# Gated mix of two attentions on one core: half sums of keys formed before the projection stretch, row halves six products apart, small copies on GpSimd, first weight loads ahead

## The chip, the cores and the metric

The kernel runs on one core of a Trainium2 chip. The metric is the device time in microseconds of one execution; lower is better. The engines are TensorE (PE in the profile, with PEld for its weight loads), VectorE (DVE), ScalarE (ACT), GpSimd (POOL) and the queue engine SyncE (SP). Each works through its own instructions in order, and waits on semaphores for the others.

## The reference

Both branches read the same x (2048 x 512) and have 32 heads of 16 columns. Branch A looks at 8 keys per query, at distances 0, 2, .. 14. Branch B has one head of keys and values for all 32 query heads, and looks at all 2048 keys.

```python
g = sigmoid((x * gate_w).sum(-1))
# A: qkv = x @ wqkv; logits over idx = pos - [0, 2, .. 14], masked below 0
a = softmax(q . k[idx] * scale) . v[idx] @ wo_a
# B: q = x @ wq (32 heads), k = x @ wk, v = x @ wv (one head)
b = softmax(q k^T * scale) v @ wo_b
out = g * a + (1 - g) * b
```

All arrays are float32. Products that need the accuracy are made of three float32r products of high and low parts.

## The kernel before

**Two row halves.** Most products have 64 rows of contraction or fewer. TensorE then works as two halves, rows 0 to 63 and rows 64 to 127, which run side by side: a product in one half and a product in the other take the time of one. Instructions are issued in one order, so a product that waits holds back those behind it in both halves.

**Start, to about 24 us.** x is loaded and split into high (`xh`, ACT) and low parts (`xl`, DVE; for the second quarter of x on POOL, `split_x(1, nc.gpsimd)`). `keys(t)` makes the keys, values and gate logits of four blocks of 512 rows in 128-row products; keys land in `kst`, and a turned copy in `turned_k` for values and gates. Two query lumps are made here, too. After it `values_of` copies pieces of `turned_k` into `vst` and `gate`: 16 pairs of small copies (L251 and L253), on ACT.

**The front stretch, 24 to 279 us (`front_stream`).** 62 lumps, 14 of queries (`queries`) and 48 of branch A's projection (`a_project`), of 12 products in each row half (L1212), accumulate into four banks `pe`. A finished bank is read by ACT: L277 and L278 for queries (`qraw`, `qhi`), L315 for branch A (`stage`). The weights of branch A come in pieces: `load_wa` issues a DMA on the POOL queue into one of two `waraw` buffers (L168), ACT makes the high part (`wah`, L119), POOL the low part (`wal`, L179).

**Max products.** The softmax of branch B subtracts the true row maximum, so all scores are made once for their maxima: 2048 products of 128 queries by 512 keys, in 32 units of 64. `max_mm` (L382) makes scores, and DVE reduces them into the tile `mx` of the unit (L420 for a pair over bank `pm`, L432 for one in bank `ps` or `po`). `unit_tile` clears the `mx` of this unit and the next, in the front on ACT (L376). The other way goes through half sums: `half_keys` (L460, 128-row products with the selector `sel`) makes half the sum and half the difference of two key blocks, ACT and DVE put them into `kcd` (L468, L472). Then max(a, b) is the half sum plus the size of the half difference: a product with the difference into `pm` is read by ACT (L511, Abs into `dd`), a product with the sum into `ps` or `po` (L481) by one DVE instruction that adds `dd` and keeps the maximum (L529). It takes as many products on TensorE and less of DVE. Before, `half_sel` builds `sel` on DVE at the eighth query lump, and `half_keys` runs for both groups of keys after it.

**The loop, 282 to 1434 us.** 512 steps (32 units of 16 key tiles). A step has two exponent pairs (`exp_pair`, two products side by side at L574, one ACT exponential of 128 x 1024 at L576) and one group of weighted sums (`weighted`, L584, four tiles of 32 columns, two passes each). Max products that the front left over go into the steps: a pair over `pm` in nearly every step, and a single one in `ps` in some. At steps 272 and 416 come blocks of output rows (`out_phase`), with more max products among them.

**What sets the order.** The kernel is recorded by a planner in Python: it keeps a clock for each engine (`clk`), adds fixed costs (`T_R` for a product slot, `T_RED1`, `T_RED2` and others for what reads a bank), and places a max product when its bank is free by that clock. In the loop `single_share` spreads what is left evenly. `FRONT` (596) ends new half-sum groups in the front when so many max products are done. What a wait really costs is not in the plan.

```python
elif at[b] < n * many and may(b, *lines[b][at[b]]):
    mm(b, lines[b][at[b]])
```

Of the kernel before, what the change touches and what calls it, by code (L numbers as in the profile page):

```python
# [13 lines left out]
P = 128  # L14
# [33 lines left out]
WB = 6  # L48


T_R, T_LAT, T_EXP, T_RED2, T_RED1, T_W, T_TTR = 0.23, 0.20, 0.92, 1.14, 0.61, 1.21, 0.70
# [34 lines left out]
def gated_mix_kernel(ctx, tc, xt, wa, wk, wq, wo_a, wo_b, out):  # L86
# [40 lines left out]
    def after(eng, ready, dur):  # L127
        clk[eng] = max(clk[eng], ready) + dur
        return clk[eng]
# [91 lines left out]
    nc.vector.memset(mk[:, 6:7], -FMAX)  # L221
    clear(0, nc.vector)
# [25 lines left out]
    def values_of(t, q):  # L248

        v = turned_k[32:64, t].rearrange("p (j b z) -> p j b z", b=4, z=32)[:, :, q, DH:2 * DH]  # L250
        nc.scalar.activation(vst[32 * q:32 * q + 32, 4 * t:4 * t + 4, 0:DH], v, AF.Copy)  # L251
        g = turned_k[96:128, t].rearrange("p (j b z) -> p j b z", b=4, z=32)[:, :, q, DH]
        nc.scalar.activation(gate[32 * q:32 * q + 32, 1, 4 * t:4 * t + 4], g, AF.Copy)  # L253
        after("act", clk["pe"], 0.45)
# [56 lines left out]
    def a_post(gg, j, bank):  # L311

        settle("store", 2)
        own = p1.tile([P, GN], F32, name="stage", bufs=4)
        nc.scalar.activation(own, bank, AF.Copy)  # L315
        at = after("act", clk["pe"] + T_LAT, 0.52)

        def store():
            for piece in a_pieces(gg):
                a_store(own, gg, j, *piece)  # L320

        tasks.append((at + 0.5, store, (), "store"))
        if j == NJ - 1:
            tasks.append((at + 1.0, whole, (gg,)))
# [32 lines left out]
    slots = [(0, pr, t, kc) for kc in range(2) for pr in range(2) for t in range(4)]  # L357
    slots += [(0, pr, t, kc) for pr in range(2) for t in range(4) for kc in range(2, 4)]
# [78 lines left out]
    sel, dd, formed, ended, wants = [], [], {}, set(), []  # L437
    hb = {}

    def half_sel():  # L440

        whole_k = wp.tile([P, 2, DH], F32, name="wholek", bufs=1)
        nc.vector.tensor_add(whole_k, twin[:, :, 0, :, 0], twin[:, :, 0, :, 1])
        sel.append(p0.tile([P, 2, P], F32R, name="sel", tag="wkh", bufs=1))
        dd.extend(p1.tile([P, 2, 512], F32, name="dd", bufs=2) for _ in range(2))
        for x in range(2):
            to = sel[0][:, x].rearrange("p (b h z) -> p b h z", b=2, h=2)
            nc.vector.tensor_scalar(to[:, :, 0].rearrange("p b (d s) -> p b d s", s=2), whole_k.unsqueeze(3).to_broadcast([P, 2, DH, 2]), 0.5 - x, 0.0, op0=ALU.mult, op1=ALU.add)
            nc.vector.tensor_scalar(to[:, :, 1].rearrange("p b (s d) -> p b s d", s=2), whole_k.unsqueeze(2).to_broadcast([P, 2, 2, DH]), 0.5 - x, 0.0, op0=ALU.mult, op1=ALU.add)
        after("dve", 0, 1.0)  # L450

    def half_keys(g):

        hb[g] = (m2.shape(2)[:, 0, :], m2[:, 1, :])
        keys = ("m2", "m2")
        clk["pe"] = max(clk["pe"], free["m2"])
        mark("m20", "m21")
        for x in range(2):
            for y in range(2):
                nc.tensor.matmul(hb[g][x], sel[0][:, x * y], kst[:, (2 * g + y) * 512:(2 * g + y + 1) * 512], start=(y == 0), stop=(y == 1))  # L460
        clk["pe"] += 1.2
        for k in keys:
            free[k] = clk["pe"] + 4.0
        tasks.append((clk["pe"] + 1.0, half_parts, (g, keys)))

    def half_parts(g, keys):
        for x in range(2):
            nc.scalar.activation(kcd[:, g, x], hb[g][x], AF.Identity, scale=mk[:, 0:1])  # L468
            at = after("act", clk["pe"], 0.65)
        for x in range(2):  # L470
# [724 lines left out]
    def mm(b, at):  # L1195
# [22 lines left out]
    ends_at, posted, first = {}, set(range(-4, 0)), {}  # L1218
# [10 lines left out]
    def front_stream():  # L1229
# [11 lines left out]
        while min(at) < n * many:  # L1241
# [16 lines left out]
            for b in sorted((0, 1), key=lambda b: b not in lone):  # L1258
# [4 lines left out]
                elif at[b] < n * many and may(b, *lines[b][at[b]]):  # L1263
# [3 lines left out]
            if lone or moved:  # L1267
                idle = 0
                after("pe", 0, T_R)
# [65 lines left out]
    free.update({f"f{k}": 0.0 for k in range(4)})  # L1335
    front_stream()
# [172 lines left out]
```

## Time and profile before

| | |
|---|---|
| median of 3 runs | 1445.83 us (1444.48 to 1447.59) |
| the profiled execution, its own time | 1444.96 us |
| its span | 1443.0 us |
| busy in the span: PE, ACT, DVE, POOL | 99%, 90%, 80%, 67% |
| granted TensorE clock | 0.999 |
| start, front stretch, first 256 steps | to 24 us, 24 to 279 us, 282 to 803 us |

The 1.96 us between the span and the time lie outside the recorded instructions. PE counts as busy while any product is in flight, and a product is in flight for about 0.4 us though the next in its half can begin 0.23 us later; so PE at 99% does not say that no product waited. The distance between the starts of products says it.

### The profile page before, as it was taken

Reading aid. Unit: us, or ns where it says so; the run is one execution under the profiler, and the core shown is the slowest. Engines: PE = TensorE matmul, PEld = TensorE weight load, DVE = VectorE, ACT = ScalarE, POOL = GpSimd, SP = SyncE. Lnnn points to the kernel's source line nnn. Section 1 sums busy time; section 2 is a strip of 40 time slices with the busy share of each in tenths; the row PEclk is TensorE's granted clock in tenths of the full one; section 3 lists DMA queues with packets and bytes.
Section 4 is the critical chain, followed back from the end, with each engine's and each line's share of the span. In section 5 each row is a group of like instructions: output and inputs, shape, how many; then the busy total and the mean of one; then the engine's idle time right before and its main releaser. Section 6 shows DMA issues by size and latency. Waiting matters only on the chain.

```text
span 1443.0 us, 29289 instructions
## 1 busy us (share of the span) xinstructions
PE 1432.9 (99%) x10524; PEld 675.9 (47%) x10524; DVE 1152.0 (80%) x1883; ACT 1297.3 (90%) x1649; POOL 963.9 (67%) x1749
## 2 busy tenths in 40 slices
PE   9999999999999999999999999999999999999998
PEld 7877767533333333333333367333333336333343
DVE  8788888788887888888888889788888888788712
ACT  5599888899999999999999988999999998999986
POOL 4541778878898898988988898888888706011220
PEclk9999999999999999999999999999999999999999
DMA  6654533402121110112322210321201011000110
GB/s 228 185 138 111 150 105 91 131 16 87 40 59 48 52 61 2 61 46 68 101 77 67 73 35 31 94 57 42 72 16 69 12 41 35 9 1 2 30 30 30
DMA packets 106969, 94.01 MB, mean 65 GB/s; under 512 B 84880, under 2 KB 89016, under 8 KB 102728
## 3 DMA queue, kind: packets, MB, share of 16 engines
q1 hardware_dynamic: 99864, 52.95, 13.5%
q0 software_dynamic: 6240, 37.89, 8.0%
q8 instruction: 82, 1.34, 0.4%
q10 hardware_dynamic: 720, 1.31, 0.3%
q14 instruction: 63, 0.52, 0.1%
HBM read 62.13 MB, written 29.45 MB: 63 GB/s over the span
## 4 chain that ended last, share of the span: by engine, by line
PE 97%; DMA 1%; ACT 1%; DVE 1%; issue 0%; SPq 0%; POOL 0%; ACTq 0%; POOLq 0%; DVEq 0%
PE po L584 35%; PE pe L574 24%; PE pe L1212 11%; PE pm L382 8%; PE ps L382 5%; PE pe L889 4%; PE pm L481 4%; PE ps L481 2%; PE po L481 2%; PE pm L943 1%; DMA qd<-qhi 0%; ACT pexp L576 0%; PE pe L238 0%; DMA waraw<-wa 0%; PE po L204 0%
## 5 line engine op out<-in xcount | busy, mean ns | idle before, releaser
L576 ACT ACTIVATE pexp<-pe 128x1024 f32<-128x1024 f32 x1022 | 983.2, 1022 | 62.8 <-PE pe L574 60.3
L420 DVE TENSOR_REDUCE mx<-pm 128x2 f32<-128x1024 f32 x486 | 594.9, 1224 | 169.3 <-PE pm L382 162.8
L584 PE MATMUL po<-pexp,vst 128*32 128x512 f32 x4096 | 545.6, 605 | 0.2 <-ACT pexp L576 0.2
L574 PE MATMUL pe<-qst,kst 64*128 64x512 f32 x1788 | 421.7, 455 | 1.7 <-ACT stage L315 0.9
L574 PEld LDWEIGHTS pe<-qst,kst 64*128 64x128 f32 x1788 | 167.6, 183 | 443.7 <-ACT pexp L576 436.6
L432 DVE TENSOR_REDUCE mx<-ps 128x1 f32<-128x512 f32 x303 | 206.2, 681 | 2.6 <-PE ps L382 2.5
L382 PE MATMUL pm<-kst,qst 62*128 62x512 f32 x915 | 186.0, 396 | 0.1
L648 POOL TENSOR_TENSOR pr<-aext 128x256 f32<-128x256 f32 x256 | 181.8, 738 | 4.7 <-DMA aext<-ad 4.5
L711 POOL TENSOR_TENSOR oa<-oa,av 128x256 f32<-128x256 f32 x224 | 164.1, 733 | 15.3
L511 ACT ACTIVATE dd<-pm 128x512 f32<-128x512 f32 x254 | 147.8, 602 | 25.1 <-PE pm L481 5.9
L584 PEld LDWEIGHTS po<-pexp,vst 128*32 128x32 f32 x4096 | 80.7, 108 | 145.2 <-issue 135.8
L708 POOL TENSOR_TENSOR av<-aext,lg 128x256 f32<-128x256 f32 x224 | 139.3, 622 | 12.9
L1212 PE MATMUL pe<-wah,xl 64*128 64x512 f32 x384 | 131.3, 396 | 0.0
L1212 PE MATMUL pe<-wal,xh 64*128 64x512 f32 x384 | 131.0, 395 | 0.0
L1212 PE MATMUL pe<-wah,xh 64*128 64x512 f32 x384 | 129.4, 395 | 0.0
L481 PE MATMUL pm<-kcd,qst 62*128 62x512 f32 x288 | 113.7, 401 | 0.1
L382 PE MATMUL ps<-kst,qst 62*128 62x512 f32 x285 | 112.6, 395 | 0.0
L529 DVE CUSTOM_DVE_ANT_0 dd<-ps,dd 128x512 f32<-128x512 f32 x127 | 87.6, 690 | 17.1 <-PE ps L481 10.1
L529 DVE CUSTOM_DVE_ANT_0 dd<-po,dd 128x512 f32<-128x512 f32 x127 | 87.7, 691 | 11.5 <-PE po L481 7.3
L382 PEld LDWEIGHTS pm<-kst,qst 62*128 62x128 f32 x915 | 88.8, 186 | 2.6 <-DVE mx L420 0.9
L654 POOL TENSOR_TENSOR tr<-pr 128x512 f32<-128x512 f32 x64 | 81.8, 1279 | 4.2
L611 POOL TENSOR_TENSOR rl<-rl,gate_t 128x16 f32<-128x16 f32 x31 | 6.9, 222 | 115.3 <-DVE rl L605 76.0
(205 smaller groups left out, 1997.0 us busy)
## 6 DMA issues: line engine op xcount, KB each, us to landing
aext<-ad POOLq DMA_DIRECT2D x32, 1056.0 KB, 5.5
ad<-stage SPq DMA_DIRECT2D x32, 240.0 KB
qst<-qd SPq DMA_DIRECT2D x56, 128.0 KB
qd<-qhi SPq DMA_DIRECT2D x16, 256.0 KB
qd<-qlo SPq DMA_DIRECT2D x16, 256.0 KB
td<-raw SPq DMA_DIRECT2D x32, 128.0 KB
oa<-td SPq DMA_DIRECT2D x256, 16.0 KB
xraw<-xt SPq DMA_DIRECT2D x15, 256.0 KB
```

The source lines that it names most:

```text
L382: nc.tensor.matmul(dst, qst[home(v)[0]][b:b + 62, pr, t * P:(t + 1) * P], kst[b:b + 62, kc * 512:(kc + 1) * 512], start=True, stop=True)
L420: nc.vector.tensor_reduce(m[:, :, pr, t, kc], dst, AX.X, ALU.max)
L432: nc.vector.tensor_reduce(m[:, odd, pr, t, kc:kc + 1], dst, AX.X, ALU.max)
L481: nc.tensor.matmul(dst, qst[home(v)[0]][b:b + 62, pr, t * P:(t + 1) * P], kcd[b:b + 62, kc // 2, x, :], start=True, stop=True)
L511: nc.scalar.activation(d[:, odd], m2[:, odd, :], AF.Abs)
L529: nc.vector.tensor_tensor_reduce(d[:, odd], dst, d[:, odd], 1.0, -FMAX, ALU.add, ALU.max, m[:, odd, pr, t, kc:kc + 1])
L574: nc.tensor.matmul(bank[:, odd, :], kst[b:b + 64, kt * P:(kt + 1) * P], qst[home(u)[0]][b:b + 64, pr, :], start=True, stop=True)
L576: nc.scalar.activation(e, bank, AF.Exp, scale=SCALE)
L584: nc.tensor.matmul(po[32 * i:32 * i + 32, :], vst[:, kt, :], pexp[s, i // 2][:, i % 2, :], start=(kt == 0), stop=(kt == NJ - 1))
L648: nc.gpsimd.tensor_mul(pr[:, k], q, e[:, o:o + NH, AC:2 * AC])
L711: nc.gpsimd.tensor_add(ao, ao, av)
L1212: nc.tensor.matmul(front_bank(x), l[h], r[h], start=(not second and i == 0), stop=(second and i == 3 * C - 1))
```

## The change

Seven things are changed, all of them in the front stretch or ahead of it.

1. `sel` (now `halves_of`) is built on DVE among the constants at the start, not in the stretch; `half_sel` is gone.
2. `half_keys` is asked for as soon as `front_stream` begins: the group of the first two key blocks stands right behind `keys(3)`, the other follows when `pm` is free. Its two ACT copies are issued with the products, not as a later task. The order of unit 0's max products (`slots`) is arranged to match.
3. Row half 1 begins only when row half 0 is six products ahead (`LAG`).
4. `values_of` copies on POOL, not on ACT; `unit_tile` clears `mx` on POOL, always.
5. The first two weight pieces of branch A are loaded ahead of `front_stream`.
6. A front step counts 0.235 in the plan (`T_F`), where it counted 0.23.
7. A weight group counts as landed when all 16 of its lumps have been stored, in whichever order.

```diff
+LAG = 6
-T_R, T_LAT, ... = 0.23, 0.20, ...
+T_F, T_R, T_LAT, ... = 0.235, 0.23, 0.20, ...
...
     def ahead_wa(gg, k):
-        if 0 <= k < 2 * C and k % 2 == 0:
+        if (4 if gg == 0 else 0) <= k < 2 * C and k % 2 == 0:
             load_wa(gg, k // 2)
...
     nc.vector.memset(mk[:, 6:7], -FMAX)
+    whole_k = cp.tile([P, 2, DH], F32, name="wholek")
+    halves_of = cp.tile([P, 2, P], F32R, name="sel")
+    nc.vector.tensor_add(whole_k, twin[:, :, 0, :, 0], twin[:, :, 0, :, 1])
+    for x in range(2):
...
     clear(0, nc.vector)
...
     def values_of(t, q):
-        nc.scalar.activation(vst[32 * q:32 * q + 32, 4 * t:4 * t + 4, 0:DH], v, AF.Copy)
+        nc.gpsimd.tensor_copy(vst[32 * q:32 * q + 32, 4 * t:4 * t + 4, 0:DH], v)
-        nc.scalar.activation(gate[32 * q:32 * q + 32, 1, 4 * t:4 * t + 4], g, AF.Copy)
-        after("act", clk["pe"], 0.45)
+        nc.gpsimd.tensor_copy(gate[32 * q:32 * q + 32, 1, 4 * t:4 * t + 4], g)
+        pool = max(pool, 1e3 * clk["pe"]) + 500
...
-        if j == NJ - 1:
+        landed[gg] = landed.get(gg, 0) + 1
+        if landed[gg] == NJ:
             tasks.append((at + 1.0, whole, (gg,)))
...
-    slots = [(0, pr, t, kc) for kc in range(2) for pr in range(2) for t in range(4)]
-    slots += [(0, pr, t, kc) for pr in range(2) for t in range(4) for kc in range(2, 4)]
+    slots = [(0, 0, t, 2 * g + kc) for g in range(2) for t in range(2) for kc in range(2)]
+    slots += [(0, pr, t, kc) for pr in range(2) for t in range(4) for kc in range(4) if pr or t > 1]
...
                 mx[x] = wp.tile([P, 2, 2, 4, 4], F32, name="mx", bufs=3)
-                if pe:
-                    nc.gpsimd.memset(mx[x], -FMAX)
-                    charge(250)
-                else:
-                    nc.scalar.activation(mx[x].rearrange("p b i t k -> p (b i t k)"), ident[:, 0:64], AF.Identity, scale=0.0, bias=mk[:, 6:7])
+                nc.gpsimd.memset(mx[x], -FMAX)
+                charge(250)
...
     def half_keys(g):
...
         clk["pe"] += 1.2
-        for k in keys:
-            free[k] = clk["pe"] + 4.0
-        tasks.append((clk["pe"] + 1.0, half_parts, (g, keys)))
-
-    def half_parts(g, keys):
         for x in range(2):
             nc.scalar.activation(kcd[:, g, x], hb[g][x], AF.Identity, scale=mk[:, 0:1])
             at = after("act", clk["pe"], 0.65)
+        for k in keys:
+            free[k] = at + 4.0
+        tasks.append((at, half_parts, (g, keys)))
...
-            if lump == ("q", 9):
-                half_sel()
-            elif lump == ("q", 10):
-                wants.extend((1, 0))
...
-                elif at[b] < n * many and may(b, *lines[b][at[b]]):
+                elif at[b] < n * many and (b == 0 or at[0] >= LAG) and may(b, *lines[b][at[b]]):
...
-                after("pe", 0, T_R)
+                after("pe", 0, T_F)
...
+    dd.extend(p1.tile([P, 2, 512], F32, name="dd", bufs=2) for _ in range(2))
+    wants.extend((0, 1))
+    for c in range(2):
+        load_wa(0, c)
     front_stream()
```

The lines of the changed kernel have other numbers: L382 is L388, L460 is L454, L481 is L476, L1212 is L1203, L123 is L124, L168 is L169.

On POOL, from the end of its clearing at the start on, the kernel before has this (`xl` are the low parts of the second quarter of x, `qlo` those of queries, `waraw` the weight pieces):

```order
L1035 MEMSET vst 128x16x16
L123 TENSOR_TENSOR xl<-xraw,xh 128x512 x4
L283 TENSOR_TENSOR qlo<-qraw,qhi 128x512 x2
L168 DMA waraw<-wa 128x512
L283 TENSOR_TENSOR qlo<-qraw,qhi 128x512 x3
L179 TENSOR_TENSOR wal<-waraw,wah 128x512
L168 DMA waraw<-wa 128x512
```

The changed kernel has this at the same place:

```order
L1030 MEMSET vst 128x16x16
L124 TENSOR_TENSOR xl<-xraw,xh 128x512 x4
L169 DMA waraw<-wa 128x512 x2
L381 MEMSET mx 128x64 x2
L259 COPY vst<-turnedk 32x4x16
L261 COPY gate<-turnedk 32x4
```

Both weight loads moved up to the four `xl`, and the two clears of `mx` and the small copies, which were on ACT, now stand behind them.

On PE, at the beginning of the front stretch, the kernel before has this, the names in brackets being engines that the row waits for (`DMAHW`: a transfer; `pe_95` and `pe_94` are banks of the first two lumps in row half 1 and 0):

```order
L382 MATMUL ps<-kst,qst_77 128x512 [waits DMAHW2_49,DMAHW1_49]
L1212 MATMUL pe_95<-xh,wqh 128x512 [waits Activation_49]
L382 MATMUL pm<-kst,qst_77 128x512
L382 MATMUL pm<-kst,qst_77 128x512 [waits DMAHW4_49,DMAHW3_49]
L382 MATMUL po<-kst,qst_77 128x512
L1212 MATMUL pe_94<-xh,wqh 128x512 [waits DVE_49]
```

In the changed kernel the four products of L454 for the first half sums stand here, and then this follows:

```order
L388 MATMUL ps<-kst,qst_77 128x512 [waits DMAHW2_49,DMAHW1_49]
L388 MATMUL po<-kst,qst_77 128x512 [waits DMAHW4_49,DMAHW3_49]
L1203 MATMUL pe_94<-xh,wqh 128x512 [waits DVE_49,Activation_49]
L1203 MATMUL pe_94<-xl,wqh 128x512
L1203 MATMUL pe_94<-xh,wql 128x512
L1203 MATMUL pe_94<-xh,wqh 128x512
L1203 MATMUL pe_94<-xl,wqh 128x512
L1203 MATMUL pe_94<-xh,wql 128x512
L1203 MATMUL pe_95<-xh,wqh 128x512 [waits Activation_49]
L1203 MATMUL pe_94<-xh,wqh 128x512
L1203 MATMUL pe_95<-xl,wqh 128x512
L388 MATMUL ps<-kst,qst_77 128x512 [waits DVE_49]
```

Six products of row half 0 now run alone, and the second product into `ps` stands some eight slots behind the first. It waits for DVE's reduction of the first one, and that reduction, which waited for PE and ACT, now waits for PE and POOL (the clear of `mx`).

More of the change, by code (lines that the diff above doesn't have):

```diff
@@ L48 @@
 WB = 6
-T_R, T_LAT, T_EXP, T_RED2, T_RED1, T_W, T_TTR = 0.23, 0.20, 0.92, 1.14, 0.61, 1.21, 0.70
+LAG = 6
+T_F, T_R, T_LAT, T_EXP, T_RED2, T_RED1, T_W, T_TTR = 0.235, 0.23, 0.20, 0.92, 1.14, 0.61, 1.21, 0.70
 class Banks:
@@ L434, in fill_one @@
         filled(v, 1)
-    sel, dd, formed, ended, wants = [], [], {}, set(), []
+    dd, formed, ended, wants = [], {}, set(), []
     hb = {}
[L440 to L450, printed above, removed]
     def half_keys(g):
@@ L459, in half_keys @@
             for y in range(2):
-                nc.tensor.matmul(hb[g][x], sel[0][:, x * y], kst[:, (2 * g + y) * 512:(2 * g + y + 1) * 512], start=(y == 0), stop=(y == 1))
+                nc.tensor.matmul(hb[g][x], halves_of[:, x * y], kst[:, (2 * g + y) * 512:(2 * g + y + 1) * 512], start=(y == 0), stop=(y == 1))
         clk["pe"] += 1.2
-        for k in keys:
-            free[k] = clk["pe"] + 4.0
-        tasks.append((clk["pe"] + 1.0, half_parts, (g, keys)))
-    def half_parts(g, keys):
         for x in range(2):
@@ L469, in half_parts @@
             at = after("act", clk["pe"], 0.65)
+        for k in keys:
+            free[k] = at + 4.0
+        tasks.append((at, half_parts, (g, keys)))
+    def half_parts(g, keys):
+        at = clk["pe"]
         for x in range(2):
@@ L1216, in mm @@
         return T_R
-    ends_at, posted, first = {}, set(range(-4, 0)), {}
+    ends_at, posted, first, landed = {}, set(range(-4, 0)), {}, {}
     def front_bank(x):
```

4 lines of the change are left out of this document (added).

## The prediction

> **What bounds the kernel now.** I read the page first, then the busy times by stage, then PE's timeline within the stages, and last the engines that PE waits for.
>
> ```profile
> PE 97%; DMA 1%; ACT 1%; DVE 1%; issue 0%; SPq 0%; POOL 0%; ACTq 0%; POOLq 0%; DVEq 0%
> ```
>
> The chain that ended last is PE's own sequence from one end to the other. So time can only come from two places: fewer product slots, or shorter waits between them. Busy times by stretch (span's start to the left, then sum and count for each engine, clock, DMA):
>
> ```profile
> core 0: us, PE busy (x) PEld busy (x) DVE busy (x) ACT busy (x) POOL busy (x), PEclk, DMA share, GB/s
> 24.00:60.00 36.00, 34.02 (x278) 31.55 (x278) 31.58 (x45) 20.19 (x57) 18.02 (x16) 1.00 0.57 163
> 60.00:100.00 40.00, 39.92 (x326) 30.11 (x326) 31.53 (x85) 31.32 (x65) 21.08 (x22) 1.00 0.54 152
> 100.00:180.00 80.00, 80.00 (x684) 60.69 (x682) 70.39 (x210) 72.60 (x145) 33.58 (x56) 1.00 0.46 127
> 180.00:278.00 98.00, 97.78 (x783) 67.95 (x781) 84.48 (x252) 82.00 (x154) 79.14 (x155) 1.00 0.35 98
> 282.00:803.00 521.00, 521.00 (x3730) 193.86 (x3722) 432.40 (x520) 494.77 (x531) 442.05 (x848) 1.00 0.20 58
> ```
>
> Two products, one in each row half, make a slot. From 100 to 180 us, 684 products are 342 slots, so a slot takes 80 / 342 = 0.234 us; from 180 to 278 us it takes 98 / 391.5 = 0.250 us, though PE counts as busy in both. The difference is waiting inside the stretch. In the loop the starts on PE's timeline tell more (start, duration, line, operands):
>
> ```profile
> 285.69 1.07 PE L584 MATMUL po<-pexp,vst 128*32 128x512 f32 x8
> 286.69 0.50 PE L574 MATMUL pe<-qst,kst 64*128 64x512 f32 x2
> 287.02 0.39 PE L382 MATMUL pm<-kst,held 62*128 62x512 f32 x2
> 287.25 0.40 PE L574 MATMUL pe<-qst,kst 64*128 64x512 f32 x2
> 287.58 1.07 PE L584 MATMUL po<-pexp,vst 128*32 128x512 f32 x8
> ...
> 289.71 1.07 PE L584 MATMUL po<-pexp,vst 128*32 128x512 f32 x8
> ```
>
> A step with only the pair of max products lasts 287.58 - 285.69 = 1.89 us, one with a single product into `ps` on top, the next in the order, 289.71 - 287.58 = 2.13 us. So a single costs 0.24 us, if ACT can follow, which these rows tell:
>
> ```profile
> 401.08 3.84 ACT L576 ACTIVATE pexp<-pe 128x1024 f32<-128x1024 f32 x4 [0.19 <-PE pe L574]
> ```
>
> ```profile
> L576 ACT ACTIVATE pexp<-pe 128x1024 f32<-128x1024 f32 x492 | 472.7, 1022 | 25.1 <-PE pe L574 23.6 <-PE pm L382 0.9
> L678 ACT ACTIVATE lg<-lg 128x128 f32<-128x128 f32 x18 | 5.6, 312 | 0.0
> ```
>
> Four exponentials in a row take 3.84 us, the last of them 1.02; so they follow each other every (3.84 - 1.02) / 3 = 0.94 us, and two per step are 1.88. A step without a single is thus at ACT's pace, too. So far such steps nearly always stand next to one with a single, which gives ACT 0.25 us of slack.
>
> **The change part by part.** The sum is made against the profiled execution, 1444.96 us (its span and 1.96 us around it); it lies 0.87 under the median of the runs, 1445.83.
>
> *Slots of the front.* Counted in the order of both programs, the stretch holds 1488 projection products and 8 half-sum products either way, and 564 max products before, 599 now. I place each product in the first free slot of its half, not ahead of the one issued before it. That makes 1039 slots before and 1060 now, with the four half-sum products that moved to its head: 17.5 slots are the 35 products, the rest are halves left empty by the lead of six. 21 x 0.234 = +4.9 us.
>
> *A new wait at its head.* Now `mx` is cleared on POOL, behind four `xl` and two weight loads:
>
> ```profile
> 13.49 0.33 POOL L1035 MEMSET vst<- 128x256 f32 x1
> 23.44 5.52 POOL L123 TENSOR_TENSOR xl<-xraw,xh 128x512 fp32r<-128x512 f32 x4 [9.61 <-ACT xh L119]
> ...
> 94.86 1.11 POOL L168 DMA_DIRECT2D waraw<-wa  x2
> ```
>
> ```profile
> 26.91 0.66 DVE L432 TENSOR_REDUCE mx<-ps 128x1 f32<-128x512 f32 x1
> ```
>
> Before, ACT cleared both tiles, and DVE, busy with keys until then, began its first reduction at 26.91. Now POOL is through with `xl` at 23.44 + 5.52 = 28.96 and with two loads at 30.07; the clear of 128x64 costs between nothing and the 0.33 of a 128x256 one, I take 0.13. So the first reduction runs from about 30.2 to 30.9. When does PE need it?
>
> ```profile
> 24.18 0.50 PE L382 MATMUL ps<-kst,qst 62*128 62x512 f32 x1
> ...
> 24.52 1.00 PE L382 MATMUL pm<-kst,qst 62*128 62x512 f32 x2
> 25.06 0.49 PE L1212 MATMUL pe<-xh,wqh 64*128 64x512 f32 x1
> ...
> 53.93 1.20 PE L460 MATMUL pm<-kst,sel 128*128 128x512 f32 x4
> 55.05 0.49 PE L382 MATMUL po<-kst,qst 62*128 62x512 f32 x1
> ```
>
> The stretch begins at 24.18. The half-sum products take 55.05 - 53.93 = 1.12, the first two max products one slot, and seven products of row half 0 stand ahead of the second product into `ps`: 24.18 + 1.12 + 8 x 0.234 = 27.2. PE is issued in order, so everything behind that product waits, in both halves, and ACT, DVE and POOL get no new banks: 30.9 - 27.2 = +3.7 us. The bounds are +0.4 (the clear in time, the reduction still at 26.91 to 27.57) and +3.9 (a clear of 0.33).
>
> *Two waits that go.* Row half 0 has two products from 24.18 to 25.06, 0.88 us where two slots are 0.47; the product between waits for a transfer of `qst`. Now half-sum products fill this time: -0.4. The other wait:
>
> ```profile
> 57.13 0.63 ACT L119 ACTIVATE wah<-waraw 128x512 fp32r<-128x512 f32 x1 [2.89 <-DMA waraw<-wa]
> ...
> 58.79 0.50 PE L1212 MATMUL pe<-xh,wqh 64*128 64x512 f32 x1 [1.83 <-ACT qhi L278]
> ```
>
> ACT waits for the second weight piece until 57.13, with the copies of a finished bank queued behind, and PE stands still for 1.83 us. Now the load of that piece is issued by 30.07: -1.8. The third and fourth piece still wait for a buffer, but stand several ACT copies ahead of their use. Front: 4.9 + 3.7 - 0.4 - 1.8 = +6.4 us.
>
> *Small copies, `sel`, `half_keys` tasks.* Taken at nothing. The cover for `sel` on DVE at the start is a wait:
>
> ```profile
> 7.73 0.69 DVE L123 TENSOR_TENSOR xl<-xraw,xh 128x512 fp32r<-128x512 f32 x1 [1.17 <-ACT xh L119]
> ```
>
> ```profile
> L449 DVE TENSOR_SCALAR sel<-wholek 128x64 fp32r<-128x64 f32 x1 | 0.2, 190 | 0.0
> ```
>
> Four such and a smaller one are under 1 us, and DVE waits 1.17 us for x before 7.73; without that cover they would delay the low parts of x by 1 us. The copies:
>
> ```profile
> L511 ACT ACTIVATE dd<-pm 128x512 f32<-128x512 f32 x37 | 21.3, 603 | 2.7 <-PE pm L481 0.9 <-PE pe L1212 0.4
> ...
> L251 ACT ACTIVATE vst<-turnedk 32x64 f32<-32x64 f32 x16 | 4.1, 255 | 0.2
> L253 ACT ACTIVATE gate<-turnedk 32x4 f32<-32x4 f32 x16 | 3.3, 205 | 0.2
> ```
>
> ACT loses 4.1 + 3.3 us, and gains Abs readings: among the first 372 projection products stand 110 half-sum products now and 32 before, so 39 more differences of 0.603, 23.5 us. In the kernel before they end near 83 us (468 products with the others among them, 278 of them by 60 us and 190 of the 326 after it). Until then ACT is busy for 20.2 + 190/326 x 31.3 = 38.4 us; it becomes 38.4 - 7.4 + 23.5 = 54.5 us of 59 + 6.4 = 65, or 0.83. That is less than the 72.60 / 80 = 0.91 at which a slot takes 0.234, so ACT covers it. POOL has 18 of 36 us free from 24 to 60, and the copies are read only at 282 us.
>
> *First 256 steps.* By the order, 145 of them had three max products and 110 two; now 112 and 143. 33 singles less are 33 x 0.24 = -7.9 us at PE's price. At ACT's mean duration, 2 x 1.022 = 2.04 for a step without a single, they would be 33 x (2.13 - 2.04) = -3.0. The pace of 0.94 is nearer to the first price; but 44 steps without a single now follow such a step (1 before), and there ACT has no slack behind which, say, the exponentials of branch A (18 x 312 ns in 500 us) could hide. I take -6.0.
>
> *After them.* Both programs hold 825 max products there. The two blocks of rows have 242, not 253, 11 halves of a slot: -1.3; and the steps 11 more at 0.24: +2.6. Together +1.3.
>
> Sum: 6.4 - 6.0 + 1.3 = +1.7 us, 1446.7 against 1444.96, and 1447.5 against the median. About 0.2%, 2.9 us, is what a measurement of this kernel can tell from no change; +1.7 is within.
>
> **The rivals.** *ACT sets the pace of the lighter loop.* From a mean of 1.96 us for a step without a single on, the singles that left are worth 3, not 6 us; the front's loss stays. Time 1447.5 + 3.0 = 1450.5, slower. For it: ACT is busy for 494.77 of 521 us there, with no slack between two such steps. Against it: 0.94 us from one exponential to the next.
>
> *The front loses its inner waits.* The lead of six products parts the copies of two finished banks, and the plan's longer step may move readings apart. If the stretch from 180 to 278 us came to 0.234 a slot, that is 391.5 x 0.0164 = 6.4 us, and 1441.1, faster. Against it: in the order the differences stand as close as before, a product into the same half of `pm` after six slots in most cases, and these waits are of that kind:
>
> ```profile
> PEld pm L481 <- ACT dd L511: 16.2, 60, 0.5
> ```
>
> *The clear is in time*, because POOL comes to it sooner than the rows say: then 0.4 in place of 3.7, and 1444.2, no change. Against it: `xl` waits for ACT, which nothing here moves.
>
> *Reading the banks limits the denser start.* If ACT could not take the Abs readings beside the products, the 23.5 - 7.4 = 16.1 us would count in place of the 4.9: 1447.5 + 11.2 = 1458.7. Against it stands the share of 0.83. [...]
>
> **How the numbers follow.** Forecast 0.48: mostly no change (0.37), at its upper end slower (0.11). ACT's pace 0.24: slower 0.20, same 0.04. Inner waits gone 0.16: faster 0.14, same 0.02. Clear in time 0.07: same 0.06, faster 0.01. Bank reading 0.05: slower. Faster 0.15, same 0.49, slower 0.36. The range runs from the second rival, 1441.0, to 2 us above the first, 1452.5, which takes in the front's bounds; it leaves out the last rival and the ends of the others, below 0.2.
>
> **What would show it.** Right: PE idle near 27 to 31 us, released by DVE after POOL's clear; no idle of PE near 57 us; the loop's first exponent pair 5 to 8 us later than before; steps without a single near 1.90 us. Wrong: the head of the front without a gap (the wait), a slot after 180 us under 0.245 (the inner waits), steps without a single at 1.96 or more (ACT's pace).

## The result, and the profile after

| | before | changed |
|---|---|---|
| median | 1446.44 us (4 runs) | 1461.77 us (3 runs, 1461.72 to 1463.93) |
| the profiled execution, its span | 1444.96, 1443.0 us | 1461.72, 1459.9 us |

A fourth run of the changed kernel was disturbed (3258.7 us) and is left out. The ratio is 1.0113 with an interval of 1.0096 to 1.013, so the change costs 14 to 19 us. The forecast was 1447.5 us, with a range from 1441.0 to 1452.5; the time lies 9 us above even its upper end.

Busy times by stretch of the changed kernel, which answer to those of before (the loop starts 12 us later, so its row does, too):

```profile
core 0: us, PE busy (x) PEld busy (x) DVE busy (x) ACT busy (x) POOL busy (x), PEclk, DMA share, GB/s
24.00:60.00 36.00, 32.16 (x238) 24.77 (x238) 26.65 (x58) 20.21 (x38) 17.91 (x44) 0.95 0.41 112
60.00:100.00 40.00, 40.00 (x327) 29.23 (x323) 29.51 (x92) 36.09 (x73) 23.07 (x24) 1.00 0.57 156
100.00:180.00 80.00, 79.05 (x664) 58.42 (x662) 70.05 (x207) 71.57 (x142) 28.07 (x51) 1.00 0.47 131
180.00:278.00 98.00, 96.62 (x782) 68.36 (x784) 84.17 (x251) 81.75 (x154) 79.35 (x156) 1.00 0.36 98
294.00:815.00 521.00, 520.16 (x3679) 190.15 (x3673) 409.09 (x480) 492.65 (x529) 437.19 (x835) 1.00 0.19 57
```

The first row has 238 products where it had 278, and its granted clock is 0.95. The last has 3679 for 3730: in the same 521 us the loop gets fewer products done.

To place the difference, the products of each trace were put against their order. The front's 1488 projection products are cut into eighths of 186; the loop is measured from its first weighted group to that 255 steps later.

| us | before | changed | difference | forecast |
|---|---|---|---|---|
| end of the first eighth | 51.3 | 61.9 | +10.7 | |
| eighths two to four | 95.4 | 94.6 | -0.8 | |
| eighths five to eight | 131.7 | 134.1 | +2.4 | |
| front, sum | 278.4 | 290.6 | +12.2 | +6.4 |
| first 255 steps | 519.0 | 521.5 | +2.5 | -6.0 |
| from there to the last product | 637.7 | 639.4 | +1.7 | +1.3 |

The head of the front, on POOL, DVE and PE of the changed kernel (start, duration, line, operands; in brackets the idle time before and who ended it):

```profile
23.34 5.43 POOL L124 TENSOR_TENSOR xl<-xraw,xh 128x512 fp32r<-128x512 f32 x4 [9.52 <-ACT xh L120]
28.73 1.16 POOL L169 DMA_DIRECT2D waraw<-wa  x2
29.88 0.25 POOL L381 MEMSET mx<- 128x64 f32 x2
```

```profile
30.08 0.69 DVE L438 TENSOR_REDUCE mx<-ps 128x1 f32<-128x512 f32 x1 [3.19 <-POOL mx L381]
```

```profile
26.60 0.39 PE L1203 MATMUL pe<-xh,wqh 64*128 64x512 f32 x1
30.83 0.75 PE L388 MATMUL ps<-kst,qst 62*128 62x512 f32 x1 [3.84 <-DVE mx L438]
...
31.38 0.63 PE L1203 MATMUL pe<-xl,wqh 64*128 64x512 f32 x1
31.39 0.63 PE L1203 MATMUL pe<-xh,wqh 64*128 64x512 f32 x1
31.81 0.63 PE L1203 MATMUL pe<-xh,wql 64*128 64x512 f32 x1
```

The wait is where the prediction put it, with its cause and size: 3.84 us for 3.7. What it didn't have stands behind it. Products start 0.43 us apart and last 0.63 us, where they had 0.23 and 0.39. The stretch by microseconds tells why:

```profile
30.00:31.00 1.00, 0.17 (x2) 0.17 (x4) 0.92 (x2) 0.00 (x0) 0.82 (x6) 0.95 0.82 139
31.00:32.00 1.00, 1.00 (x6) 0.82 (x8) 0.75 (x2) 0.00 (x0) 0.83 (x5) 0.50 1.02 344
32.00:33.00 1.00, 1.00 (x8) 0.82 (x6) 1.00 (x3) 0.00 (x0) 0.84 (x5) 0.50 1.05 209
33.00:34.00 1.00, 1.00 (x8) 0.73 (x7) 1.00 (x2) 0.00 (x0) 0.10 (x1) 0.50 0.13 29
34.00:35.00 1.00, 1.00 (x10) 0.66 (x6) 0.87 (x2) 0.00 (x0) 0.00 (x0) 0.84 0.00 0
```

The clock that was granted (third column from the right) is 0.50 for 3.4 us after the wait. By an estimate from the 0.50 and the 3.4 us, half of that time, 1.7 us, is lost; pe_filled below measures 1.9.

In the loop, this is PE's timeline over two steps without a single product, between two that hold one:

```profile
597.96 1.06 PE L579 MATMUL po<-pexp,vst 128*32 128x512 f32 x8
598.96 0.50 PE L569 MATMUL pe<-held,kst 64*128 64x512 f32 x2
599.29 0.40 PE L388 MATMUL pm<-kst,qst 62*128 62x512 f32 x2
599.53 0.40 PE L569 MATMUL pe<-held,kst 64*128 64x512 f32 x2
599.86 1.07 PE L579 MATMUL po<-pexp,vst 128*32 128x512 f32 x8
600.85 0.50 PE L569 MATMUL pe<-held,kst 64*128 64x512 f32 x2
601.19 0.40 PE L388 MATMUL pm<-kst,qst 62*128 62x512 f32 x2
601.55 0.50 PE L569 MATMUL pe<-held,kst 64*128 64x512 f32 x2
601.98 1.06 PE L579 MATMUL po<-pexp,vst 128*32 128x512 f32 x8
```

```profile
599.56 3.83 ACT L571 ACTIVATE pexp<-pe 128x1024 f32<-128x1024 f32 x4 [0.20 <-PE pe L569]
603.58 1.94 ACT L571 ACTIVATE pexp<-pe 128x1024 f32<-128x1024 f32 x2 [0.19 <-PE pe L569]
```

The first such step lasts 599.86 - 597.96 = 1.90 us. The second lasts 2.12 us, as long as a step that holds a single: its second exponent pair starts 0.36 us after the pair into `pm`, not 0.24 us, and its weighted group comes 0.43, not 0.33 us behind that pair. ACT's row has the same sum: four exponentials take 3.83 us and 0.19 us of waiting for PE, 4.02 = 1.90 + 2.12. So it looks as if a step of 1.90 us were only possible behind a longer one, and a single product in every second step were free. Counted over the first 255 steps, 107 are shorter than 2.0 us before, and 107 after, though there are 33 fewer with a single. The experiments test this.

### The profile page after: what moved, and what is told of

It is laid out like the page before. It is cut to its first block, busy times and chain, and to the rows that moved or that the text cites. A ratio compares the mean times of both kernels' runs of the same rounds, so it can differ in the third digit from the quotient of the medians.

```text
span 1459.9 us, 29388 instructions
## 1 busy us (share of the span) xinstructions
PE 1443.1 (99%) x10524; PEld 671.1 (46%) x10524; DVE 1138.9 (78%) x1890; ACT 1305.1 (89%) x1638; POOL 970.5 (66%) x1790
## 4 chain that ended last, share of the span: by engine, by line
PE 91%; POOL 2%; DVE 2%; DMA 2%; issue 1%; ACT 1%; SPq 0%; ACTq 0%; DVEq 0%; POOLq 0%
PE po L579 34%; PE pe L569 23%; PE pe L1203 9%; PE pm L388 8%; PE pe L884 4%; PE ps L388 4%; PE pm L476 4%; PE ps L476 2%; PE po L476 1%; PE pm L938 1%; POOL pr L643 1%; DVE mx L426 1%; POOL tr L649 0%; ACT pexp L571 0%; DMA wqr<-wq 0%
## 5 line engine op out<-in xcount | busy, mean ns | idle before, releaser
L426 DVE TENSOR_REDUCE mx<-pm 128x2 f32<-128x1024 f32 x479 | 586.3, 1224 | 189.0 <-PE pm L388 182.7
L506 ACT ACTIVATE dd<-pm 128x512 f32<-128x512 f32 x292 | 169.7, 605 | 31.5 <-PE pm L476 9.2
L388 PE MATMUL pm<-kst,qst 62*128 62x512 f32 x921 | 185.1, 397 | 0.5 <-DVE mx L426 0.2
L438 DVE TENSOR_REDUCE mx<-ps 128x1 f32<-128x512 f32 x266 | 181.0, 680 | 3.5 <-POOL mx L381 3.2
L1203 PE MATMUL pe<-wal,xh 64*128 64x512 f32 x384 | 130.4, 397 | 0.0
L1203 PE MATMUL pe<-wah,xl 64*128 64x512 f32 x384 | 128.8, 395 | 0.0
L1203 PE MATMUL pe<-wah,xh 64*128 64x512 f32 x384 | 128.7, 395 | 0.0
L476 PE MATMUL pm<-kcd,qst 62*128 62x512 f32 x302 | 121.0, 405 | 1.3 <-ACT dd L506 1.1
L524 DVE CUSTOM_DVE_ANT_0 dd<-ps,dd 128x512 f32<-128x512 f32 x146 | 100.7, 690 | 24.5 <-PE ps L476 10.1
L524 DVE CUSTOM_DVE_ANT_0 dd<-po,dd 128x512 f32<-128x512 f32 x146 | 100.9, 691 | 14.0 <-PE po L476 7.6
L388 PE MATMUL ps<-kst,qst 62*128 62x512 f32 x261 | 103.8, 398 | 3.8 <-DVE mx L438 3.8
L388 PEld LDWEIGHTS pm<-kst,qst 62*128 62x128 f32 x921 | 87.8, 186 | 3.7 <-DVE mx L426 2.5
## 6 DMA issues: line engine op xcount, KB each, us to landing
qst<-qd SPq DMA_DIRECT2D x56, 128.0 KB
td<-raw SPq DMA_DIRECT2D x32, 128.0 KB
```

Of the source, the lines that this page charges most:

```text
L388: nc.tensor.matmul(dst, qst[home(v)[0]][b:b + 62, pr, t * P:(t + 1) * P], kst[b:b + 62, kc * 512:(kc + 1) * 512], start=True, stop=True)
L426: nc.vector.tensor_reduce(m[:, :, pr, t, kc], dst, AX.X, ALU.max)
L438: nc.vector.tensor_reduce(m[:, odd, pr, t, kc:kc + 1], dst, AX.X, ALU.max)
L476: nc.tensor.matmul(dst, qst[home(v)[0]][b:b + 62, pr, t * P:(t + 1) * P], kcd[b:b + 62, kc // 2, x, :], start=True, stop=True)
L506: nc.scalar.activation(d[:, odd], m2[:, odd, :], AF.Abs)
L524: nc.vector.tensor_tensor_reduce(d[:, odd], dst, d[:, odd], 1.0, -FMAX, ALU.add, ALU.max, m[:, odd, pr, t, kc:kc + 1])
```

## The experiments

Unless it says otherwise, each starts from the changed kernel (1461.7 us), and times are medians; in brackets stands the ratio to the kernel before, with its 95% interval. The kernel before took 1445.4 to 1445.8 us beside them.

**The clear ahead of `xl`** (clear_first).

```diff
+    unit_tile(0)
     split_x(1, nc.gpsimd)
```

> The changed kernel (1461.8 us) with one edit: the two clears of mx stand on POOL ahead of the four xl, where POOL has waited for nothing but xh for 9.5 us. Theory W (the wait at the head costs twice: 3.84 us of idle time, of which about 0.4 stays, and then 3.4 us at a granted clock of 0.50, which is 1.7 us of lost products): both go, 1461.8 - 3.4 - 1.7 = 1456.7. Rival (the wait costs its length only, the slow products behind it are late for another reason): 1458.4, and the products behind 27 us still start 0.4 us and more apart. Rival of the prediction (the denser start is limited by the readers of the banks): the time that is won at the head is lost again before 100 us, 1460 or more.

Measured: 1456.27 us (1.0072, 1.0059 to 1.0084). The clears are on POOL at 13.74 now, and PE's row at the place of the wait, with the slot after it:

```profile
27.09 0.49 PE L388 MATMUL ps<-kst,qst 62*128 62x512 f32 x1 [0.38 <-DVE mx L438]
27.09 0.50 PE L1204 MATMUL pe<-xh,wql 64*128 64x512 f32 x1
27.43 0.39 PE L1204 MATMUL pe<-xl,wqh 64*128 64x512 f32 x1
...
27.66 0.39 PE L1204 MATMUL pe<-xh,wql 64*128 64x512 f32 x1
```

Of 3.84 us 0.38 stays, and the products behind it are 0.23 us apart. The first eighth ends at 56.6 instead of 61.9 us. Theory W holds, and nothing is given back later: the remaining seven eighths take 228.9 us, 228.7 before the edit.

**Products that nobody reads, in the wait** (pe_filled).

```diff
+        if dst is m1 and not pe:
+            lones[0] += 1
+            if lones[0] == 2:
+                for i in range(14):
+                    nc.tensor.matmul(eb[0][:, 0, :], halves_of[:, 0], kst[:, 0:512], start=True, stop=True)
```

> The changed kernel (1461.8 us) with 14 products that nobody reads (128 rows, 0.28 us each, 3.9 us) put into a bank that is not yet in use, ahead of the product into ps that waits for the clear of mx. The wait itself stays. Theory (a wait of this length makes the granted clock fall to 0.50 for 3.4 us): PE stays at work, the clock stays at 1.00, the products behind 30.8 us start 0.23 us apart, and 3.4 x 0.5 = 1.7 us come back: 1460.1. Rival (the products behind the wait are slow because of what they wait for): no change, 1461.8, and the granted clock between 31 and 34 us is 0.50 as before.

Measured: 1457.64 us (1.0081, 1.0067 to 1.0095).

```profile
26.74 3.53 PE L441 MATMUL pe<-kst,sel 128*128 128x512 f32 x14
30.56 0.49 PE L388 MATMUL ps<-kst,qst 62*128 62x512 f32 x1 [0.29 <-DVE mx L444]
30.57 0.50 PE L1209 MATMUL pe<-xh,wql 64*128 64x512 f32 x1
30.90 0.39 PE L1209 MATMUL pe<-xl,wqh 64*128 64x512 f32 x1
```

The product into `ps` starts at 30.56, where it started at 30.83, but the clock stays at 1.00. These are the four microseconds behind it, first in the changed kernel, then here:

```profile
31.00:35.00 4.00, 4.00 (x22) 3.04 (x22) 3.62 (x6) 0.00 (x0) 1.78 (x9) 0.59 0.55 145
```

```profile
31.00:35.00 4.00, 4.00 (x30) 2.80 (x28) 3.32 (x7) 0.91 (x2) 1.57 (x8) 1.00 0.48 123
```

The first eighth is 1.9 us shorter. So the lost clock is a cost of its own, shown apart from the wait. The time fell by 4.1 us, more than expected. In the traces the other part lies at the loop's first step: 3.65 us in the changed kernel, at a clock of 0.50, and 2.11 here. What happens there is told in the last section.

**Single products put back** (singles_back; 30 of them in the trace).

```diff
+                run[0] = 0 if one else run[0] + 1
+                if not one and run[0] % 2 == 0 and 0 < s < 255:
+                    nc.tensor.matmul(m1, qst[home(u)[0]][0:62, 0, 0:P], kst[0:62, 0:512], start=True, stop=True)
+                    nc.vector.tensor_reduce(unread, m1, AX.X, ALU.max)
```

> The changed kernel (1461.8 us) with a single max product and its DVE reduction, which nobody reads, added to every second step of a run of steps without a single, in the first 255 steps: about as many as the 33 that the change took out of these steps. Theory P (two steps in a row take at least 4.02 us because of PE and ACT waiting for each other; a step without a single behind another such one lasts 2.12 us, as if it held a single): the added ones lie in that waiting and cost nothing, 1461.8 +- 0.7. The prediction's price (0.24 us each): +7.9, 1469.7. ACT's mean price (0.09 each): +3.0, 1464.8.

Measured: 1461.58 us (1.0111, 1.0097 to 1.0124). The same two steps as above, now with an added product (L1409):

```profile
599.86 1.06 PE L579 MATMUL po<-pexp,vst 128*32 128x512 f32 x8
600.85 0.50 PE L569 MATMUL pe<-held,kst 64*128 64x512 f32 x2
601.19 0.40 PE L388 MATMUL pm<-kst,qst 62*128 62x512 f32 x2
601.42 0.39 PE L1409 MATMUL ps<-kst,held 62*128 62x512 f32 x1
601.56 0.49 PE L569 MATMUL pe<-held,kst 64*128 64x512 f32 x2
601.98 1.07 PE L579 MATMUL po<-pexp,vst 128*32 128x512 f32 x8
```

The product lies in the waiting, and the step lasts 2.12 us with it as without it. The median didn't move. In the traces the sum of the 255 steps is helped by a first step of 2.12 for 3.65 us; without it, the 254 others take 519.5 for 517.8 us, 1.6 us for 30 products or 0.05 each. Both prices of the prediction (0.24 and 0.09) fall.

**The same singles, two steps running** (clumped).

```diff
+        if s < 255:
+            need = 1.3 if bare[0] else -1.0 if twice[0] == 1 else 9.0
...
+        twice[0] = twice[0] % 2 + 1 if not bare[0] else 1
```

> The changed kernel (1461.8 us) with the same number of max products in the first 255 steps (619) and the same front, but the single ones placed in two steps running, followed by steps without one, where the planner spreads them. Theory P (a step of 1.90 us is possible only behind one of 2.12): by the order 86 steps can be such fast ones, where it was 111, so 25 x 0.23 = +5.7, 1467.5. The prediction's view (a single costs the same wherever it stands): no change, 1461.8.

Measured: 1469.08 us (1.0164, 1.015 to 1.0178), so +7.4 in the median; the trace is of a run of 1471.64 us, +9.9. In it 83 of the 255 steps are short, where 107 were, and without the first step the others take 522.3 for 517.8 us: 4.4 us for 24 short steps fewer. The first step is 0.6 us shorter. Of the rest of the 9.9, 1.9 us lie in the front, whose slow clock behind the wait lasted 6.8 us this time, 2.1 us behind the 255 steps and 2.1 us behind the last product. So in these steps the same work is dearer by its placement. In all 16 traces of this case no step under 2.0 us stands behind another such one among the first 255, and the shortest two neighbours together take 3.99 us.

**The lead taken away** (lag0), and **with the clear first and singles apart** (clear_lag_apart).

```diff
-LAG = 6
+LAG = 0
...
+    unit_tile(0)
     split_x(1, nc.gpsimd)
...
-    need = ... 0.3 if bare[0] else 0.5 if (s + 1) % NJ == 0 else 1.0
+    need = ... -1.0 if bare[0] else 0.5 if (s + 1) % NJ == 0 else 1.3
```

(The first hunk alone is lag0.)

> The changed kernel (1461.7 us) with the lead of row half 0 taken away (0 for 6 products). By the order the front has 10 slots fewer, 126 for 136 in its first eighth and the others alike: -2.3; in the first 255 steps 114 for 111 fast steps, after them 83 for 94, and 6 products fewer in the blocks of rows: -0.7 + 2.5 - 0.7. The wait for the clear stays. Theory (the lead costs its empty slots and nothing else): 1461.7 - 1.2 = 1460.5, the end of the front 2.3 us earlier. Rival (the lead also makes the waits inside the front longer): the front 4 us shorter or more, and 1458.5 or less.

> The changed kernel with the clears ahead of xl (1456.3 us), no lead, and the planner's thresholds for single products moved so that they stand apart rather than together. By the order 10 slots fewer in the front (-2.3), 116 fast steps for 111 in the first 255 and 95 for 94 after them (-1.4): 1452.6. Rival (a single costs the same wherever it stands): 1454.0. Either way it stays above the kernel before, 1445.8, by the longer waits inside the front and the fuller first eighth of it.

Measured: 1450.41 us (1.0038, 1.0025 to 1.005) and 1445.43 us (0.9997, 0.9988 to 1.0006). Both are far better than expected; the rival of lag0 had the direction. The singles set apart are worth little: 113 short steps for 109 in lag0, and 0.8 us of the 254 steps behind the first. From clear_first to clear_lag_apart the front ends 6.9 us earlier, of which 5.7 us lie in eighths five to eight, though it has 537 slots there for 534. PE's waits for ACT's reading of differences, in the whole trace (total us, times, longest), are first those of the changed kernel and then those of lag0:

```profile
PEld pm L476 <- ACT dd L506: 22.2, 74, 1.2
...
PE pm L476 <- ACT dd L506: 2.6, 11, 0.8
```

```profile
PEld pm L476 <- ACT dd L506: 9.5, 38, 0.9
```

And the late front of lag0, 826 products where the changed kernel has 782:

```profile
180.00:278.00 98.00, 97.81 (x826) 71.72 (x824) 89.71 (x267) 85.49 (x163) 85.05 (x167) 1.00 0.40 108
```

That is 98 / 413 = 0.237 us a slot, for 0.251. PE's own such waits fall from 2.6 us in 11 to 0.5 us in one. So in the changed kernel the inner waits come with the lead and go with it: eighths five to eight take 134.1 us with it, 128.5 without it, and took 131.7 before. In the second half of the front a difference follows the one before it in its half after five or six slots 112 times with the lead and 119 times without, so it is not the distance in the order. That ACT's copies of the two banks, parted by the lead, now delay two readings instead of one, is only argued. On the kernel before, the lead has no such effect (loads_lead below), so it takes the rest of the order to bring it about.

**Early weight loads alone, on the kernel before** (loads_alone).

```diff
-        if 0 <= k < 2 * C and k % 2 == 0:
+        if (4 if gg == 0 else 0) <= k < 2 * C and k % 2 == 0:
...
+    for c in range(2):
+        load_wa(0, c)
     front_stream()
```

> The kernel before (1445.8 us) with one part of the change: the first two weight pieces are loaded ahead of the front stretch. By the order the products stay where they were. Theory (the prediction's step): ACT no longer waits 2.89 us for the second piece, so PE's wait of 1.83 us near 57 us goes, and nothing is late next: 1445.8 - 1.8 = 1444.0. Rival (the next copy or bank is late there instead): 1445.8, with a PE wait of 1 us or more somewhere between 55 and 70 us.

Measured: 1442.48 us (11 runs), a ratio of 0.9983 (0.9974 to 0.9992). The wait at 57 us is gone and nothing is late next; from 24 to 60 us PE does 291 products for 278:

```profile
24.00:60.00 36.00, 35.66 (x291) 30.65 (x290) 34.05 (x48) 19.70 (x56) 17.54 (x16) 1.00 0.60 169
```

The front ends 2.1 us earlier. This is the only version that is shown to beat both kernels, the one before by 0.17%.

**Half sums earlier** (halves_earlier), **the lead** (loads_lead) and **the longer step** (loads_step), **each alone, on loads_alone.**

```diff
-            if lump == ("q", 9):
+            if lump == ("q", 5):
...
-            elif lump == ("q", 10):
+            elif lump == ("q", 6):
```

```diff
-                elif at[b] < n * many and may(b, *lines[b][at[b]]):
+                elif at[b] < n * many and (b == 0 or at[0] >= LAG) and may(b, *lines[b][at[b]]):
```

```diff
-                after("pe", 0, T_R)
+                after("pe", 0, 0.235)
```

> As loads_alone, and the half sums of keys are asked for four query lumps earlier, all else as in the kernel before (no lead between the row halves, clears and small copies on ACT). By the order: front 2 slots fewer (-0.5), one more fast step in the first 255 (-0.2), 8 fewer after them (+1.8), 13 fewer products in the blocks of rows (-1.5). Theory (earlier half sums as such bring no waits): 1444.0 - 0.4 = 1443.6. Rival (the waits of about 3 us more in the changed kernel's front come from the early half sums, their readers being late): 1446.6, and the stretch after 60 us is longer by 2 us and more.

> The kernel before with the early weight loads (1442.5 us) and the lead of six products between the row halves, nothing else. By the order the front keeps its 563 max products and its slots (1040 for 1039), the first 255 steps their pattern (110 for 109 fast ones), the blocks of rows have 8 products fewer (-0.9). Theory L (a lead of six makes the products into pm wait for ACT's readings of it, at any state of the rest): the eighths five to eight of the front, 131.7 us before, get 4 us longer and more, 1446 or more. Rival S (the lead by itself costs nothing, it is the 35 more max products of the changed front that it doesn't suit): 1441.6 to 1442.5.

> The kernel before with the early weight loads (1442.5 us), and a front step counted 0.235 in the plan instead of 0.23, nothing else. By the order 9 max products more in the front and 5 slots (+1.2), 117 fast steps for 109 in the first 255 (-1.8), 84 for 98 after them (+3.2), 22 products fewer in the blocks of rows (-2.6): 1442.5. Theory (the longer step in the plan puts the products into pm where ACT has read them, so waits inside the front go, as in the stretch of 0.237 us a slot of the changed kernel without the lead): eighths five to eight 2 to 4 us shorter than the 130.7 that they take without it, 1439 to 1440.5. Rival (the step in the plan changes no waits): 1442.5.

Measured: 1455.78 us (1.007, 1.0058 to 1.0083), 1451.43 (1.0046, 1.0032 to 1.006) and 1456.71 (1.008, 1.0066 to 1.0094). Each lost 9 to 14 us against loads_alone. Two expectations had the direction (the rival of halves_earlier, theory L of loads_lead), none the cause. All have a new wait of PE that ends at 182 to 186 us, and two of them one that ends at 116 and 119. In loads_lead eighths five to eight take 5.4 us more, and that wait (3.80 us) with the slow clock behind it (0.50 for 3.4 us, 1.7 by estimate) makes 5.5: the lead by itself made no inner waits longer there, and theory L had its direction by luck. In halves_earlier, on ACT, POOL and PE:

```profile
179.87 0.60 ACT L315 ACTIVATE stage<-pe 128x512 f32<-128x512 f32 x1 [0.39 <-PE pe L1212]
184.62 0.63 ACT L119 ACTIVATE wah<-waraw 128x512 fp32r<-128x512 f32 x1 [4.15 <-DMA waraw<-wa]
```

```profile
179.80 1.30 POOL L179 TENSOR_TENSOR wal<-waraw,wah 128x512 fp32r<-128x512 f32 x1
181.04 0.58 POOL L168 DMA_DIRECT2D waraw<-wa  x1
```

```profile
186.02 0.79 PE L481 MATMUL pm<-kcd,qst 62*128 62x512 f32 x1 [4.14 <-ACT dd L511]
```

POOL can issue a load only when it has read the older piece in the buffer (`wal`, until 181.1), behind its work for branch A. The piece is there 3.6 us later. ACT stands at its copy all that time, the reading of `pm` stands behind it, and PE behind that. PE's clock is then 0.50 for 3.4 us once more. Whether a copy comes too early for its load depends on small shifts in the plan, and the kernel before has it once, at 57 us.

**The step of 0.23 again, without the lead** (lag0_tf23).

```diff
-LAG = 6
-T_F, T_R, ... = 0.235, 0.23, ...
+LAG = 0
+T_F, T_R, ... = 0.23, 0.23, ...
```

> The changed kernel without the lead (1450.4 us), and a front step counted 0.23 in the plan again. By the order 13 max products and 6 slots fewer in the front (-1.4), 113 for 114 fast steps in the first 255 and 84 for 83 after them, 5 products fewer in the blocks of rows (-0.6): 1448.4. Theory (the 0.235 is what keeps the products into pm from waiting): eighths five to eight at 131 us or more where they take 128.5 without the lead, 1451 and more. Rival (the 0.235 changes no waits): 1448.4.

Measured: 1451.24 us (1.0046, 1.0034 to 1.0059). Eighths five to eight take 129.6 us, and PE's waits at 120 and 186 us (1.6 us each) are again copies of weight pieces. Less the second of them it would be 128.0, where it was 128.5 with the longer step. So the step in the plan is not what keeps these eighths short.

**Weight pieces by SP's queue, three buffers** (step_sp3 on loads_step, halves_sp3 on halves_earlier, cla_sp3 on clear_lag_apart).

```diff
-        waraw[gg, c] = p1.tile([P, GN], F32, name="waraw", bufs=2)
-        nc.gpsimd.dma_start(waraw[gg, c], ...)
+        waraw[gg, c] = p1.tile([P, GN], F32, name="waraw", bufs=3)
+        nc.sync.dma_start(waraw[gg, c], ...)
```

> As loads_step (1456.7 us), but the weight pieces are loaded by SP's queue into one of three buffers, where POOL issued them behind its own work into one of two. Theory D (ACT's copies of pieces waited for loads issued late): PE's waits of 2.0 us at 119 and 2.8 us at 186 us go, and the 1.6 us lost at the lower clock behind the second: 1456.7 - 6.4 = 1450.3. What is left is the wait near 73 us, which has another cause (ACT's copy of queries waits 1.9 us for POOL). Rival (the load only coincides with late readers): 1456 or more, with the two waits at their place.

> As halves_earlier (1455.8 us), with the weight pieces loaded by SP's queue into one of three buffers. Theory D: the waits of 1.97 us at 116 and 4.31 us at 186 us go, with about 1.6 us of lower clock behind each: 1455.8 - 9.5 = 1446.3. Then asking for the half sums earlier costs next to nothing by itself. Rival (early half sums cost through late readers): 1453 or more.

> As clear_lag_apart (1445.4 us), with the weight pieces loaded by SP's queue into one of three buffers. No copy of a piece waits in its trace, so by theory D nothing comes of it: 1445.4 +- 0.8. If POOL's or SP's queue itself matters (POOL gets 0.6 us for each of 14 loads, SP's stores stand behind a load that waits for its buffer), it shows here: 1443 or less, or 1447 or more.

Measured: 1448.18 us (1.002, 1.0011 to 1.0029), 1447.99 (1.002, 1.0011 to 1.0029) and 1444.15 (0.9992, 0.9983 to 1.0). The first two get 8.5 and 7.8 us back with the same products in the same order. The copy that waited until 184.62 us in halves_earlier stands at 177.41 us now, with no idle time ahead of it:

```profile
173.87 0.63 ACT L119 ACTIVATE wah<-waraw 128x512 fp32r<-128x512 f32 x1
...
177.41 0.62 ACT L119 ACTIVATE wah<-waraw 128x512 fp32r<-128x512 f32 x1
```

So the late loads were the cause of these 8.5 and 7.8 us (theory D). The edit changes the queue and the number of buffers together, and no run parts them. Both versions stay 5.7 and 5.5 us above loads_alone, in the traces 5.2 and 2.7 us of it at the end of the front; whether the longer step and the early half sums cost that by themselves is open. The lead was not run with this edit. The control fell by 1.3 us, somewhat more than expected; its loop's first step takes 2.12 us in the trace, 3.70 without the edit.

## Why the prediction was wrong

The sum came to +1.7 us, and the trace is 16.8 us longer. Of the 15.1 us between them 8.5 lie in the first 255 steps of the loop, 5.8 in the front, 0.4 behind these steps and the last 0.4 outside the products that were placed.

- *Slots of the front, +4.9.* Right. All 21 stand in the first eighth (136 for 115), and its +10.7 us less the wait of 3.84 and the slow clock of 1.9 leave 5.0. With the 0.4 us that the `qst` wait was to give back it should be 4.5.
- *A new wait at its head, +3.7.* Right in place, chain and size. The mis-sized part is what follows it: PE's clock, which the prediction left at 1.00, costs 1.9 us more (pe_filled), and wait and clock 5.3 us together (clear_first).
- *Two waits that go, -2.2.* The larger one, 1.8, is right: PE has no wait near 57 us, and the part alone gains 2.1 us of front. In the changed kernel some of it is lost again: PE stands still for 0.77 us at 123 us, since ACT waits 1.25 us for a later weight piece, the sixth, of which the prediction says nothing.
- *The inner waits.* The prediction kept them as they were, since the order had the differences as far apart as before. They grew by 2.4 us in the last four eighths, with 534 slots as before. As a rival it gave the lead of six the merit of parting ACT's copies; in the changed kernel the lead does the opposite, by a mechanism that stays open. Its removal is worth 11.4 us in all (lag0), the largest single edit, of which the front's part is 7.0 us and the loop's first step 1.5.
- *First 256 steps, -6.0.* **This step failed**, by 8.5 us: 6.7 by the price of a single, 1.8 in the loop's first step (1.89 us before, 3.65 now at a clock of 0.50, and 2.12 in singles_back, where the clock stays at 1.00). It priced a single product at 0.24 us wherever it stands. A single costs 0.23 us only if it falls into a step that could have been short, and only every second step can. The prediction saw the pace (1.88 us for ACT, 1.89 for PE) and took the two for nearly independent. Before, singles stood in about every second step, where most cost nothing; the change took out 33 of these and left 107 short steps, as many as there were. The rival of ACT's pace had the right place, and its condition is met (143 steps without a single last 1.96 us in the mean); but its price, 0.09 for 0.24, was still too high. singles_back and clumped bear this out: a single put into the waiting costs 0.05 us, a short step lost 0.18.
- *After them, +1.3.* +1.7 in the trace, but by luck: the steps give +1.4 where +2.6 was the forecast, by the same flat price, and the two blocks of rows +0.3 where it was -1.3. *Small copies and `sel` at nothing:* no wait for either is in the trace; the copies are on POOL with 0.23 and 0.18 us each.
- *Reading the banks.* The 16 us of that rival are not there: the first eighth is explained without them, and ACT is busy for 36.09 of 40 us between 60 and 100 us while PE has no idle time.

## What to carry to other kernels

When two engines feed each other through two buffers and have nearly equal work, price an added or removed instruction by the period of the pair, over two rounds or more (here 4.02 us for two steps), and by where it falls; the difference between two neighbouring steps is not its price. A wait on PE can cost more than its length: behind the one of 3.84 us here the granted clock was 0.50 for 3.4 us, which cost 1.9 us more (pe_filled). An instruction that waits for a load, on an engine that others wait for, is a risk that a plan without landing times moves about at random: look where each such copy stands against its load in the order, or load from another queue into one buffer more, which gave back 8.5 and 7.8 us here.

## What the runs showed of the hardware

Between 24 and 300 us of all 16 traces the granted clock of PE is 1.00 or 0.50, and a drop to 0.50 lasts 3.4 us or twice that. Each of the eight waits of PE from 2.6 to 4.2 us in the front brought a drop, of 6.8 us in clumped, lag0 and lag0_tf23. Of seven waits from 1.5 to 1.9 us one did (1.80 us, halves_earlier).

The length of a wait alone does not decide. The 1.80 us of halves_earlier brought a drop; the 1.83 us in the kernel before and the 1.87 us in loads_step, near 118 us, brought none. What else decides is not shown.

At the handover to the loop PE waits for ACT twice, 0.95 and 0.71 us in the changed kernel. Six of the 16 traces have a drop there. Two that have none, pe_filled and singles_back, have the same two waits to 0.01 us, and singles_back has the front of the changed kernel unaltered. So neither the program of the front nor the length of these waits decides alone whether there is a drop at that place. In the changed kernel it is worth 1.5 us: the loop's first step takes 3.65 us with it, and 2.12 in singles_back without.
